# Attention, soft-MoE and FFN on one core: the logits' maximum, two v loads and the first chain change places, and the last first layer goes to fp16 parts

## The chip, the core and the metric

One core of a Trainium2 chip runs the whole program. Its engines are named as the profile names them: PE (TensorE matmul, with PEld for its weight loads), DVE (VectorE), ACT (ScalarE), POOL (GpSimd) and SP (SyncE, which issues nearly all DMAs). The metric is the device time of one execution in microseconds (us).

## The reference

Three layers follow each other on 4608 tokens (8 batches of 576) of 512 features.

```python
# attention: q, k, v of 8 batches x 8 heads x 576 x 64
scores = q @ k.T / sqrt(64);  mask: block of 64 rows sees blocks up to its own
attn = softmax(scores);  x = attn @ v          # 4608 x 512
# soft MoE: phi 512 x 32 slots, 8 experts of 4 slots, w1 512 x 1024, w2 1024 x 512
logits = x @ phi
d = softmax(logits, over the tokens);  slot_input = d.T @ x
slot_out[e] = relu(slot_input[e] @ w1[e]) @ w2[e]
c = softmax(logits, over the slots);   x = c @ slot_out
# FFN: w_in 512 x 2048, w_out 2048 x 512
h = relu(x @ w_in);  out = (h * h) @ w_out
```

The softmax over the tokens runs over all batches, so the kernel keeps a running maximum of the logits for each slot, and rescales what it has summed so far.

## The kernel before

The program goes through five stretches: a start-up (to about 61 us), attention (61 to 425), the experts (to 476), the FFN's first four token tiles (to 545), and the last stage, the other 32 token tiles (to the end).

Attention walks over 32 pairs of heads, four to a batch. In `pair(n)` the scores of pair n, the row maxima of pair n+2 (`maxpass`: PE `ps_max`, DVE `pm` and `ptl`, L498), the products with v of pair n-1 (`pv`: PE `xm` and `tl`), and the scaling and splitting of q and k of pair n+3 (`split`: ACT and DVE write `qa`, `ka`, `qb`, L441 and L447) are interleaved in eight slots. SP then moves `qb` by a transposing DMA (`t<-qb`, L473), `ka` by another, and loads further q, k and v. PE's order in attention is the order in which the code issues its work; that of DVE and ACT comes from a scheduler, within the dependencies. Each engine runs its own queue in order: what waits holds up what is behind it.

The soft-MoE work of batch b-1 is a list of items that the pairs of batch b take one at a time in five of their slots: five `logits` in the second pair of the batch, five more items in the third, and the rest from the fourth on. `logits(u)` ends on POOL (`lg`, `ltl`, L752); `maxes` takes the maximum on DVE (`mxb`, L802 and L803) and copies it (`mx`, L805); `running` transposes it on PE (`ps_mx`, L810) and forms the running maximum and its negative `nm`; `weights` spreads `nm` on PE (`ps_nb`, L821), after which DVE adds it to the logits (`d`, L825 and L826) and ACT takes the exponential (L829, L830); `total` sums `d` on PE (`ps_ds`, L870); `tokens(u)` transposes a tile of attention's output on PE (`ps_x`, L847) and scales it on DVE (`x`, L857). Decoding of FFN weights (`raw`, `dec_sq`, `tin`) runs on DVE and ACT beside it in the batches where it is due.

In the start-up, `prepare` writes constants into `s` on DVE by eleven operations (L294, L300), while the first q and k are squared (ACT `junk`, L382) and summed (PE `ps_ssq`, L389); `chain` turns the sums into scales on DVE (L394 to L411), which ACT's first `ka` needs.

The last stage takes 16 blocks of two token tiles. A block has seven products of 24 fp16 matmuls of 256 columns (L1520) and four groups of `block_first` for the next block: each four fp32 matmuls of 256 columns on the weights `ws` and the inputs `cts` (`ps_hb`, L1484), which ACT (L1375, L1376, L1507) and DVE (L1453, L1497) turn into the fp16 parts of the next block. A string `ORDER` fixes the queues of PE, DVE and ACT from the FFN's fifth part to the end of block 0; behind it PE's order is that of the code.

Of the kernel before, what the change touches and what calls it, by code (L numbers as in the profile page):

```python
# [23 lines left out]
def tile_attn_soft_moe_ffn(  # L24
# [23 lines left out]
    NG = 6  # L48
# [63 lines left out]
    exps = []  # L112

    def after_exp(x):
        if exps:
            tc.add_manual_dep(
                x.ins, exps[-1].ins.name,
                mybir.DependencyInfo(mybir.DependencyClass.NoSync, mybir.DependencyReason.DATA), reason="order",
            )

# [122 lines left out]
    def attention():  # L243
# [132 lines left out]
        def scale(ns, gap=0):  # L376
# [10 lines left out]
            def chain():  # L387
# [334 lines left out]
        def batch(b):  # L722
# [117 lines left out]
            def tokens(u, j0=0, j1=NJ):  # L840
# [9 lines left out]
                if j0 == NJ - 1:  # L850
# [5 lines left out]
                    return  # L856
                nc.vector.tensor_tensor(  # L857
                    out=box[u][0:w].rearrange("p (hp j d) -> p j hp d", hp=2, j=NJ)[:, j0:j1],
# [57 lines left out]
            if b == B - 1:  # L916
# [95 lines left out]
        def pair(n):  # L1012
# [259 lines left out]
    def setup_sel():  # L1272
        sel = c_p.tile([128, 4, 160], F32R, name="sel", bufs=1)
        nc.vector.memset(sel.bitcast(F32), 0.0)
        for i in range(0, 5, 2):
            nc.vector.tensor_copy(sel[:, :, 32 * i:32 * i + 32], ident.rearrange("p (c s) -> p c s", c=4))
        ident_r = c_p.tile([128, 128], F32R, name="ident_r", bufs=1)
        nc.vector.tensor_copy(ident_r, ident)
        cts["sel"], cts["id"] = sel, ident_r
        t = cts["all"] = lo_p.tile([128, 9 * 512], F32R, tag="lo", name="cts")  # L1280
        for g in range(NTILE // NG):
            cts[g] = t[:, NTOK * g:NTOK * g + NTOK]

# [12 lines left out]
    def combine_c(g):  # L1296
        e = lg[:, NG * g:NG * g + NG, :]
        cs = cts["cs_p"].tile([128, NG, 4, NSL], F32R, tag="cs", name="cs", bufs=2)
        for i in range(2):
            nc.vector.tensor_copy(cs[:, :, i, :], e)  # L1300
        for i in range(2, 4):
            nc.vector.tensor_tensor(out=cs[:, :, i, :], in0=e, in1=cs[:, :, 0, :], op=ALU.subtract)
        css[g] = cs

    def combine_b(ps, g):
        pt = ps.bitcast(F32R)
        cs = css.pop(g)
        for i in range(NG):
            nc.tensor.transpose(pt[:, 128 * i:128 * i + 128], cs[:, i].rearrange("p a s -> p (a s)"), cts["id"])
        nc.scalar.copy(cts[g], pt[:, 0:NTOK])  # L1310

    def ffn():
# [65 lines left out]
        def first_hidden(c, step=1024, late=False):  # L1378
# [5 lines left out]
            for a in range(2):  # L1384
# [4 lines left out]
                if step == 512:  # L1389
                    relu_square(ps, g[:, 512 * a:512 * a + 512], 512 * a, 512 * a + 512)  # L1390
                    if a == 0:
                        spread(2, parts[0])
            if late:
                return
            if step == 1024:
                relu_square(ps, g, 0, 1024)
            return g

        def first_square(c, ps):
            g = hid[c] = g_p.tile([128, 1024], F32, tag="g", name="g")  # L1400
            relu_square(ps, g, 0, 1024)

# [22 lines left out]
        def scale_alpha():  # L1425
# [5 lines left out]
                out=se, in0=m2[:, 1:2], scalar=2.0 ** 58, in1=m2[:, 0:1], op0=ALU.mult, op1=ALU.mult  # L1431
            )
            ts(out=se, in0=se, scalar1=2.0 ** -56, scalar2=None, op0=ALU.max)
            ts(out=se.bitcast(U32), in0=se.bitcast(U32), scalar1=MASK, scalar2=None, op0=ALU.bitwise_and)
            ts(out=sg.bitcast(U32), in0=se.bitcast(U32), scalar1=MASK, scalar2=None, op0=ALU.bitwise_xor)
            nc.vector.scalar_tensor_tensor(
                out=sc["alpha"], in0=sg, scalar=2.0 ** 63, in1=h, op0=ALU.mult, op1=ALU.mult
            )
            nc.vector.scalar_tensor_tensor(
                out=sc["inv"], in0=se, scalar=2.0 ** -12, in1=se, op0=ALU.mult, op1=ALU.mult  # L1440
            )

# [35 lines left out]
        def block_first(n, kq):  # L1478
            ps = hbs[n, kq] = bank2("ps_hb")
            c0 = T0 + 256 * n  # L1480
            for j in range(2):
                for a in range(2):
                    f = 2 * kq + j + KH * a
                    nc.tensor.matmul(  # L1484
                        ps[:, 512 * j + 256 * a:512 * j + 256 * a + 256], ws[:, 128 * f:128 * f + 128],
                        ctt[:, c0:c0 + 256], start=True, stop=True,
                    )

        def block_square(n, kq):
            ps = hbs.pop((n, kq))  # L1490
            x = a7[n, kq] = tw["a"].tile([128, 2, 7, 128], F32, tag="a7", name="a7")
            relu_square(ps, x[:, :, 0:4].rearrange("p k a x -> p k (a x)"), 0, 1024, scale=sc["alpha"][:, 0:1])

# [132 lines left out]
        with tc.manual_schedule(engines={E.PE, E.DVE, E.Activation}):  # L1626
# [79 lines left out]
```

## Time and profile before

| | us |
|---|---|
| timed runs, median | 877.38 |
| timed runs, lowest and highest | 873.22, 877.43 |
| profiled execution, its own time | 875.35 |
| profiled execution, span of its instructions | 873.6 |
| PE busy over the span | 818.8 (94%) |
| DVE busy | 668.1 (76%) |
| ACT busy | 625.4 (72%) |
| mean granted clock of TensorE | 0.981 |

An engine's busy time is what its instructions took; its share is taken over the whole span, whose stages have different limits. The rows for the stages and waits stand further below.

### The profile page before, as it was taken

The numbers are of one execution on the slowest core, as the hardware profiler recorded it, in microseconds if no ns is written. First come the engines' busy times: TensorE is split into PE (matmuls) and PEld (weight loads), VectorE is DVE, ScalarE is ACT, GpSimd is POOL, SyncE is SP. The second block draws the span as 40 slices with busy tenths as digits, with TensorE's granted clock in tenths as the row PEclk, the third lists the DMA queues.
The fourth block names the chain that finished last, engine by engine and source line by source line (L and its number), as shares of the span: only waits on it lengthen the run. The fifth ranks groups of instructions, "written<-read, shape, count | busy, mean of one in ns | idle before, by whom it ended". The sixth has DMA issues, their size and how long they took to land.

```text
span 873.6 us, 21610 instructions
## 1 busy us (share of the span) xinstructions
PE 818.8 (94%) x8725; PEld 604.0 (69%) x8725; DVE 668.1 (76%) x1539; ACT 625.4 (72%) x991; POOL 242.9 (28%) x394
## 2 busy tenths in 40 slices
PE   1779999899999999999996999999999999999997
PEld 1446767576666667677432554888898998888887
DVE  5848789989898987764824899788888888888880
ACT  4669787777778777744214889887888888878770
POOL 0236757556475757464000000000000000000000
PEclk9879999999999999999998899999999999999999
DMA  8799898989899987689999300110000000000002
GB/s 150 143 184 181 126 222 153 220 168 212 178 202 190 169 150 160 122 235 310 358 387 387 121 1 0 57 41 26 26 25 26 25 26 25 26 25 26 25 26 49
DMA packets 220356, 113.14 MB, mean 130 GB/s; under 512 B 192096, under 2 KB 194144, under 8 KB 220256
## 3 DMA queue, kind: packets, MB, share of 16 engines
q1 hardware_dynamic: 217600, 111.11, 55.0%
q8 instruction: 68, 1.11, 0.6%
q10 hardware_dynamic: 2656, 0.66, 0.4%
q14 instruction: 32, 0.26, 0.1%
HBM read 78.71 MB, written 9.44 MB: 101 GB/s over the span
## 4 chain that ended last, share of the span: by engine, by line
PE 75%; DMA 8%; POOL 5%; ACT 5%; DVE 3%; issue 2%; SPq 1%; ACTq 0%; POOLq 0%
PE ps_y L1520 14%; PE ps_x L1520 10%; PE ps_z L1520 10%; PE xm L636 7%; PE ps_sc L562 6%; PE po L1542 4%; DMA t<-qb 4%; PE ps_hb L1484 3%; POOL ul L752 2%; PE sm L656 2%; PE ps_max L484 2%; PE ps_u L743 2%; DMA wch<-in_moe_w_dram 2%; POOL ss L605 2%; PE tl L647 2%
## 5 line engine op out<-in xcount | busy, mean ns | idle before, releaser
L1520 PEld LDWEIGHTS <-ah 128*128 128x128 f16 x1792 | 170.4, 98 | 21.5
L600 ACT ACTIVATE p<-ps_sc,es 128x512 f32<-128x512 f32 x192 | 130.1, 686 | 59.8 <-PE ps_sc L562 30.5
L1453 DVE TENSOR_TENSOR al<-a,ah 128x1024 f16<-128x1024 f32 (+1 forms) x128 | 138.6, 1125 | 16.7 <-ACT ah L1507 15.3
L498 DVE TENSOR_REDUCE pm<-ps_max 128x4 f32<-128x512 f32 x160 | 106.5, 684 | 37.0 <-PE ps_max L492 36.8
L605 POOL TENSOR_TENSOR ss<-p 128x384 f32<-128x384 f32 (+1 forms) x128 | 86.0, 690 | 159.6 <-ACT p L600 159.2
L1507 ACT CAST ah<-a 128x1024 f16<-128x1024 f32 (+1 forms) x128 | 114.4, 936 | 14.9 <-DVE a L1453 13.6
L562 PE MATMUL ps_sc<-t,s 128*128 128x512 f16 (+3 forms) x512 | 107.8, 304 | 11.4 <-DMA t<-qb 6.3
L1613 POOL TENSOR_TENSOR ot<-u,p 128x256 f32<-128x256 f32 x16 | 12.5, 783 | 374.6 <-DVE u L1584 358.7
L1520 PE MATMUL ps_y<-bh,ah 128*128 128x256 f16 x384 | 104.8, 273 | 0.0
L1520 PE MATMUL ps_y<-bl,ah 128*128 128x256 f16 x384 | 104.7, 273 | 0.0
L1520 PE MATMUL ps_y<-bh,al 128*128 128x256 f16 x384 | 104.7, 273 | 0.0
L605 POOL TENSOR_TENSOR ss<-ss,p 128x320 f32<-128x320 f32 (+1 forms) x128 | 98.9, 773 | 16.1 <-ACT p L600 8.4
L1375 ACT ACTIVATE r<-ps_hb,alpha 128x1024 f32<-128x1024 f32 x64 | 71.2, 1112 | 33.7 <-PE ps_hb L1484 33.0
L1520 PEld LDWEIGHTS <-al 128*128 128x128 f16 x896 | 87.7, 98 | 10.2
L636 PE MATMUL xm<-p,ar_hi 128*64 128x256 f32 (+3 forms) x512 | 89.0, 447 | 0.0
L1453 DVE TENSOR_TENSOR a<-a 128x256 f32<-128x256 f32 x192 | 76.2, 424 | 3.9
L1520 PE MATMUL ps_x<-bh,ah 128*128 128x256 f16 x256 | 70.1, 274 | 0.0
L1520 PE MATMUL ps_z<-bh,ah 128*128 128x256 f16 x256 | 69.9, 273 | 0.0
L1520 PE MATMUL ps_x<-bl,ah 128*128 128x256 f16 x256 | 69.8, 273 | 0.0
L1520 PE MATMUL ps_x<-bh,al 128*128 128x256 f16 x256 | 69.8, 273 | 0.0
L1520 PE MATMUL ps_z<-bh,al 128*128 128x256 f16 x256 | 69.8, 273 | 0.0
L1520 PE MATMUL ps_z<-bl,ah 128*128 128x256 f16 x256 | 69.8, 273 | 0.0
(257 smaller groups left out, 1788.2 us busy)
## 6 DMA issues: line engine op xcount, KB each, us to landing
wch<-in_moe_w_dram SPq DMA_DIRECT2D x18, 1024.0 KB, 12.8
ar_hi<-in_v_dram SPq DMA_DIRECT2D x64, 128.0 KB, 3.9
raw<-in_moe_w_in_dram SPq DMA_DIRECT2D x16, 512.0 KB, 5.4
out_dram<-ot SPq DMA_DIRECT2D x32, 256.0 KB, 2.2
ar_hi<-in_moe_w_dram SPq DMA_DIRECT2D x6, 1024.0 KB, 8.9
s<-s SPq DMA_DIRECT2D x32, 144.0 KB, 4.0
ar_hi<-in_k_dram SPq DMA_DIRECT2D x16, 256.0 KB, 4.6
ar_hi<-in_q_dram SPq DMA_DIRECT2D x16, 256.0 KB, 4.7
```

The source lines that it names most:

```text
L484: nc.tensor.matmul(ps[:, c0:c0 + 128 * (u + 1)].rearrange("p (s c) -> p s c", c=128), t1[:, 2 * u + hp, :], s1[:, hp:2 * u + 2:2, :], star ...
L498: nc.vector.tensor_reduce(out=o, in_=i, axis=AX.X, op=ALU.max)
L562: nc.tensor.matmul(ps[:, c0:c0 + w].rearrange("p (s c) -> p s c", c=128), kk[:, 2 * t + hp, :], qq[:, 2 * u0 + hp:8:2, :], start=(c0 == 0 ...
L600: exps[:] = [nc.scalar.activation(out=pt, in_=ps, func=AF.Exp, scale=es[:, 0:1])]
L605: add = lambda o, x, y: nc.gpsimd.tensor_tensor(out=o, in0=x, in1=y, op=ALU.add)
L636: nc.tensor.matmul(box["xm"][64 * hp:64 * hp + 64, 128 * t:512], vs[:, t, hp, :], r, start=(t == 0), stop=(t == 3),)
L1375: nc.scalar.activation(out=r[:, c0:c1], in_=ps[:, c0:c1], func=AF.Relu, **kw)
L1453: sub = lambda o, a, b: nc.vector.tensor_tensor(out=o, in0=a, in1=b, op=ALU.subtract)
L1484: nc.tensor.matmul(ps[:, 512 * j + 256 * a:512 * j + 256 * a + 256], ws[:, 128 * f:128 * f + 128], ctt[:, c0:c0 + 256], start=True, stop=True,
L1507: nc.scalar.copy(v(hl[n % 2][0][:, 2 * kq:2 * kq + 2], s), v(a7[n, kq], s))
L1520: nc.tensor.matmul(acc[:, 0:HM], a[:, k], b[:, k], start=bool(first and k + j == 0), stop=(k == KH - 1 and j == 2), skip_group_check=not f ...
L1542: nc.tensor.matmul(pos[t], g[:, 512 * a + 128 * t:512 * a + 128 * t + 128], tt[:, c, a], start=(c == 0 and a == 0), stop=(c == KH - 1 and ...
```

## The change

It has four parts.

1. The constant writes of `prepare` are collected, and the first operation of the first chain (for pair 0) is made to come behind all of them on DVE.
2. The items change places: `tokens(1)` before `maxes`, and then `tokens(2)`, `running`, `tokens(3)`, `weights` in place of `maxes`, `tokens(1)`, `running`, `tokens(2)`, `weights`, `tokens(3)`. So `running` stands one slot later, `weights` one, `tokens(1)` to `tokens(3)` one earlier; `total` keeps its slot. In all batches but the last, `mxb` on DVE comes behind the evacuation of `tokens(1)`'s `x`.
3. In the second pair of a batch no v is loaded; the pair's v is loaded in the third instead, and the third's in the fourth, which loads its own too.
4. The first layer of blocks 2 to 15 takes fp16 inputs and weights: `combine_c` and `combine_b` leave scaled fp16 high and low parts of the inputs, `halves_w` splits the weights, and `spread_w` packs them by 16 fp16 matmuls of 512 columns and two copies of ACT, in the course of block 0. The scale of those blocks' relu changes with it. Blocks 0 and 1 keep fp32.

```diff
@@ ORDER @@
-        "o3 l10 c11 H13 P2 E5 l11 q12 P7 E2 s12 q13 P3 E7 c12 s13 c13 l12 P4 E3 l13 E4"
+        "o3 l10 c11 H13 P2 E5 l11 q12 w P7 E2 s12 q13 W0 P3 E7 c12 s13 W1 c13 l12 P4 E3 l13 E4"
@@ prepare @@
-                    nc.vector.tensor_scalar(out=o, in0=x, scalar1=SHIFT, scalar2=None, op0=ALU.mult)
+                    ready.append(nc.vector.tensor_scalar(out=o, in0=x, scalar1=SHIFT, scalar2=None, op0=ALU.mult))
@@ chain @@
-                nc.vector.tensor_scalar(out=a, in0=a, scalar1=1e-30, scalar2=None, op0=ALU.max)
+                x = nc.vector.tensor_scalar(out=a, in0=a, scalar1=1e-30, scalar2=None, op0=ALU.max)
+                if ns == [0]:
+                    for y in ready:
+                        order(x, y)
@@ batch @@
-                nc.vector.tensor_reduce(out=mxb, in_=lm.rearrange("p u s -> p s u"), axis=AX.X, op=ALU.max)
+                x = nc.vector.tensor_reduce(out=mxb, in_=lm.rearrange("p u s -> p s u"), axis=AX.X, op=ALU.max)
+                if b < B - 1:
+                    order(x, box["x"])
...
-                + [lambda: tokens(0), maxes, lambda: tokens(1), running, lambda: tokens(2), weights, lambda: tokens(3)]
+                + [lambda: tokens(0), lambda: tokens(1), maxes, lambda: tokens(2), running, lambda: tokens(3), weights]
@@ pair @@
-            if n + 2 < N:
-                dq += load_v(n + 2)
+            for m_ in {0: (n + 2,), 1: (), 2: (n + 1,), 3: (n + 1, n + 2)}[jn]:
+                if m_ < N:
+                    dq += load_v(m_)
@@ combine_c @@
-        cs = cts["cs_p"].tile([128, NG, 4, NSL], F32R, tag="cs", name="cs", bufs=2)
+        cs = cts["cs_p"].tile([128, NG, 4, NSL], F16, tag="cs", name="cs", bufs=2)
@@ ffn @@
+        wfs = cts["w"][:, p]
         nc.scalar.copy(wfs, psw[:, p])
+        nc.scalar.copy(cts["w"][:, parts[0]], psw[:, parts[0]])
...
+        def halves_w():
...
+            wh = cts["wh"].rearrange("p (i f) -> p i f", i=2)
+            nc.scalar.activation(out=wh[:, 0], in_=cts["w"], func=AF.Copy, scale=sw)
+            nc.vector.scalar_tensor_tensor(
+                out=wh[:, 1], in0=cts["w"], scalar=sw, in1=wh[:, 0], op0=ALU.mult, op1=ALU.subtract
+            )
+
+        def spread_w(k):
+            ps = bank2("ps_wh")
+            for c in range(2):
+                for i in range(4):
+                    nc.tensor.matmul(
+                        ps[32 * i:32 * i + 32, 512 * c:512 * c + 512], cts["id_h"][:, 64 * c + 32 * k:64 * c + 32 * k + 32],
+                        cts["wh"][:, 512 * (i % 2):512 * (i % 2) + 512], start=True, stop=True, tile_position=(0, 32 * i),
+                    )
+            nc.scalar.copy(
+                cts["ws"].rearrange("p (c k f) -> p c k f", c=2, k=2)[:, :, k], ps.rearrange("p (c f) -> p c f", c=2)
+            )
...
+            w, c = (ws, ctt[:, c0:c0 + 256]) if n < 2 else (cts["ws"], cts["half"][:, c0 - CT0:c0 - CT0 + 256])
             for j in range(2):
                 for a in range(2):
                     f = 2 * kq + j + KH * a
                     nc.tensor.matmul(
-                        ps[:, 512 * j + 256 * a:512 * j + 256 * a + 256], ws[:, 128 * f:128 * f + 128],
-                        ctt[:, c0:c0 + 256], start=True, stop=True,
+                        ps[:, 512 * j + 256 * a:512 * j + 256 * a + 256], w[:, 128 * f:128 * f + 128], c,
+                        start=True, stop=True,
                     )
```

What this does to the queues is seen at three places. Line numbers are those of the kernel that the rows are from; from the chain on, those of the changed kernel are 7 to 12 higher. The first place is DVE's queue in the start-up, where `cst` and `s` are the constants and `ps_ssq` the sums of the first chain; before:

```order
L293 TENSOR_TENSOR cst<-ident 64x1
L394 TENSOR_SCALAR ps_ssq<-ps_ssq 128x2
L294 SCALAR_TENSOR_TENSOR cst<-ident,cst 64x6
L300 TENSOR_SCALAR s_0_144<-cst 64x8x64
...
L300 TENSOR_SCALAR s_1_145<-cst 64x4x64
L395 TENSOR_SCALAR ps_ssq<-ps_ssq 128x2
```

And of the change:

```order
L300 TENSOR_TENSOR cst<-ident 64x1
L301 SCALAR_TENSOR_TENSOR cst<-ident,cst 64x6
L307 TENSOR_SCALAR s_0_144<-cst 64x8x64
...
L307 TENSOR_SCALAR s_1_145<-cst 64x4x64
L401 TENSOR_SCALAR ps_ssq<-ps_ssq 128x2
L405 TENSOR_SCALAR ps_ssq<-ps_ssq 128x2
```

The chain's first operation has moved behind all eleven constant writes, and its second follows it directly.

The second place is DVE's queue in the third pair of batch 2, where the work of batch 1 is taken up; before:

```order
L802 TENSOR_REDUCE mxb<-lg 128x32
L447 SCALAR_TENSOR_TENSOR qb_142<-ar_hi,sig,qa 128x9x64
L803 TENSOR_TENSOR mxb<-mxb,ltl 64x32
L805 COPY mx_2754<-mxb 128x128
L498 TENSOR_REDUCE pm_146<-ps_max 128x4
L498 TENSOR_REDUCE ptl<-ps_max 128x4
...
L857 TENSOR_TENSOR x<-ps_x,rc 128x4x2x64
L189 SCALAR_TENSOR_TENSOR tin<-dec_sq,raw 128x512
L498 TENSOR_REDUCE pm_146<-ps_max 128x4
L195 TENSOR_SCALAR dec_sq<-tin 128x512
```

And of the change:

```order
L457 SCALAR_TENSOR_TENSOR qb_142<-ar_hi,sig,qa 128x9x64
L508 TENSOR_REDUCE pm_146<-ps_max 128x4
L508 TENSOR_REDUCE ptl<-ps_max 128x4
...
L869 TENSOR_TENSOR x<-ps_x,rc 128x4x2x64
L508 TENSOR_REDUCE pm_146<-ps_max 128x4
L196 SCALAR_TENSOR_TENSOR tin<-dec_sq,raw 128x512
L812 TENSOR_REDUCE mxb<-lg 128x32
L508 TENSOR_REDUCE pm_146<-ps_max 128x4
L815 TENSOR_TENSOR mxb<-mxb,ltl 64x32
L202 TENSOR_SCALAR dec_sq<-tin 128x512
L817 COPY mx_2773<-mxb 128x128
```

`mxb` and `mx` have moved from ahead of eleven operations to behind them. On PE, `ps_mx` has changed places with the group of `ps_x` that followed it directly.

The third place is ACT's queue in the fourth pair of that batch, with the exponentials of `d`; before:

```order
L600 ACTIVATE p<-ps_sc,es 128x512
L382 ACTIVATE junk,ssq<-ar_hi 128x576
L829 ACTIVATE d<-d 64x32
L830 ACTIVATE d<-d 128x128
L600 ACTIVATE p<-ps_sc,es 128x512
L382 ACTIVATE junk,ssq<-ar_hi 128x576
L600 ACTIVATE p<-ps_sc,es 128x512 x2
```

And of the change:

```order
L610 ACTIVATE p<-ps_sc,es 128x512
L389 ACTIVATE junk,ssq<-ar_hi 128x576
L610 ACTIVATE p<-ps_sc,es 128x512
L389 ACTIVATE junk,ssq<-ar_hi 128x576
L841 ACTIVATE d<-d 64x32
L610 ACTIVATE p<-ps_sc,es 128x512
L842 ACTIVATE d<-d 128x128
L193 ACTIVATE dec_sq<-raw 128x512
```

Another `p` and `junk` stand ahead of the first `d`, and a `p` between the two. On PE, `ps_nb`, which `d` waits for, has changed places with the last full group of `ps_x`, and `ps_ds`, which waits for `d`, stands where it stood.

## Rows read from the trace of the kernel before

**Rows 1.** Windows by stage: length, busy of PE, PEld, DVE, ACT, POOL, PEclk, DMA.

```profile
61.00:425.00 364.00, 351.59 (x4881) 243.82 (x4877) 292.55 (x788) 266.30 (x542) 215.76 (x353) 1.00 0.95 193
545.00:873.00 328.00, 324.12 (x2932) 290.71 (x2930) 251.57 (x426) 249.61 (x292) 12.53 (x16) 1.00 0.09 30
```

**Rows 2.** Waits of PE, 60 to 430 us: total us, times, longest.

```profile
PE ps_sc L562 <- DVE pm L498: 4.7, 4, 1.7
PE ps_sc L562 <- DMA t<-qb: 3.6, 5, 1.6
PE ps_ssq L389 <- ACT p L600: 1.1, 5, 0.2
```

**Rows 3.** Timeline of DVE at the start: start, us, instruction, idle before it.

```profile
11.68 0.17 DVE L394 TENSOR_SCALAR ps_ssq<-ps_ssq 128x2 f32<-128x2 f32 x1 [6.32 <-PE ps_ssq L389]
...
11.83 2.00 DVE L300 TENSOR_SCALAR s<-cst 64x512 f16<-64x512 f32 x10
```

**Rows 4.** Timeline of PE, 46 to 52 us.

```profile
50.97 0.38 PE L389 MATMUL ps_ssq<-ssq,ones 128*128 128x2 f32 x2 [3.15 <-ACT junk L382]
```

**Rows 5.** Timeline of DVE, 150 to 170 us.

```profile
152.49 0.37 DVE L802 TENSOR_REDUCE mxb<-lg 128x32 f32<-128x128 f32 x1
...
154.34 0.23 DVE L805 COPY mx<-mxb 128x128 f32<-128x128 f32 x1
154.49 0.68 DVE L498 TENSOR_REDUCE pm<-ps_max 128x4 f32<-128x512 f32 x1
...
160.41 0.16 DVE L533 TENSOR_REDUCE ps_max<-pm 128x4 f32<-128x16 f32 x1
```

**Rows 6.** Timeline of PE, 155 to 175 us.

```profile
155.22 0.59 PE L562 MATMUL ps_sc<-t,s 128*128 128x512 f16 x2 [0.62 <-DVE pm L498]
...
158.05 0.28 PE L810 MATMUL ps_mx<-ident,mx 128*128 128x128 f32 x1
...
165.22 0.40 PE L821 MATMUL ps_nb<-ident,nm 32*128 32x32 f32 x2
...
167.01 0.66 PE L847 MATMUL ps_x<-ident,xt 128*128 128x128 f32 x4
...
168.28 0.39 PE L870 MATMUL ps_ds<-ones,d 128*32 128x1 f32 x10
...
173.58 0.38 PE L562 MATMUL ps_sc<-t,s 128*128 128x512 f16 x1 [1.62 <-DMA t<-qb]
```

**Rows 7.** Timeline of ACT, 164 to 171 us.

```profile
166.86 0.68 ACT L382 ACTIVATE junk<-ar_lo 128x576 fp8e4<-128x576 f32 x1
...
167.65 0.30 ACT L830 ACTIVATE d<-d 128x128 f32<-128x128 f32 x1
167.84 0.67 ACT L600 ACTIVATE p<-ps_sc,es 128x512 f32<-128x512 f32 x1
```

**Rows 8.** Timeline of SP's DMA issues, 149 to 176 us.

```profile
164.46 1.50 SPq L312 DMA_DIRECT2D ar_hi<-in_v_dram  x1
...
167.70 1.56 SPq L473 DMA_TRANSPOSE t<-qb  x1
```

**Rows 9.** Timeline of PE in a block of the last stage, 599 us on.

```profile
599.75 0.27 PE L1520 MATMUL ps_y<-bl,ah 128*128 128x256 f16 x1
```

**Rows 10.** Timeline of all engines around a first-layer group, 606.8 to 608.2 us.

```profile
607.07 0.27 PE L1520 MATMUL ps_y<-bh,al 128*128 128x256 f16 x1
...
607.10 0.71 PE L1484 MATMUL ps_hb<-cts,ws 128*128 128x256 f32 x4
...
607.77 0.27 PE L1520 MATMUL ps_x<-bl,ah 128*128 128x256 f16 x1
```

**Rows 11.** Timeline of PE in the expert stage, 471 to 475 us.

```profile
472.45 1.92 PE L1183 MATMUL psw<-tin,so 128*32 128x512 f32 x16 [0.28 <-DVE so L1176]
```

**Rows 12.** Timeline of ACT at the start of the FFN.

```profile
474.44 0.27 ACT L1349 CAST wf<-psw 128x128 fp32r<-128x128 f32 x1 [2.59 <-PE psw L1183]
```

**Rows 13.** Windows in the start-up, same columns as in rows 1.

```profile
56.00:61.00 5.00, 5.00 (x34) 2.41 (x36) 2.96 (x17) 4.03 (x8) 2.05 (x3) 0.50 1.29 217
```

More of the change, by code (lines that the diff above doesn't have):

```diff
@@ L64, in tile_attn_soft_moe_ffn @@
     NTOK = 128 * NG
+    CT0 = 128 * N0 + 512
+    CSC = 2.0 ** 15
     KF = FF // 128
@@ L112, in tile_attn_soft_moe_ffn, with order @@
     exps = []
+    def order(x, y):
+        tc.add_manual_dep(
+            x.ins, y.ins.name,
+            mybir.DependencyInfo(mybir.DependencyClass.NoSync, mybir.DependencyReason.DATA), reason="order",
+        )
+    ready = []
     def after_exp(x):
         if exps:
[L116 to L119, printed above, removed]
+            order(x, exps[-1])
     def qk_tile(b):
@@ L856, in tokens @@
                     return
-                nc.vector.tensor_tensor(
+                box["x"] = nc.vector.tensor_tensor(
                     out=box[u][0:w].rearrange("p (hp j d) -> p j hp d", hp=2, j=NJ)[:, j0:j1],
@@ L1276, in setup_sel @@
             nc.vector.tensor_copy(sel[:, :, 32 * i:32 * i + 32], ident.rearrange("p (c s) -> p c s", c=4))
[L1277 to L1282, printed above, removed]
+        cts["sel"] = sel
+        cts["all"] = c_p.tile([128, CT0], F32R, name="cts", bufs=1)
+        t = lo_p.tile([128, 9 * 512], F32, tag="lo", name="cts_h")
+        n_h = NT - CT0
+        cts["half"] = t[:, 0:n_h // 2].bitcast(F16)
+        t = t[:, n_h // 2:]
+        cts["ws"], cts["wh"] = t[:, 0:FF // 2].bitcast(F16), t[:, FF // 2:FF // 2 + 512].bitcast(F16)
+        cts["id_h"] = t[:, FF // 2 + 512:FF // 2 + 576].bitcast(F16)
+        nc.vector.tensor_copy(cts["id_h"], ident)
+        c0 = FF // 2 + 1088
+        cts["w"] = t[:, c0 - 512:c0]
+        cts["tiny"] = [t[:, c0 + i:c0 + i + 1] for i in range(4)]
     def combine_a(g):
@@ L1297, in combine_c @@
         e = lg[:, NG * g:NG * g + NG, :]
-        cs = cts["cs_p"].tile([128, NG, 4, NSL], F32R, tag="cs", name="cs", bufs=2)
+        cs = cts["cs_p"].tile([128, NG, 4, NSL], F16, tag="cs", name="cs", bufs=2)
         for i in range(2):
-            nc.vector.tensor_copy(cs[:, :, i, :], e)
+            nc.vector.tensor_scalar(out=cs[:, :, i, :], in0=e, scalar1=CSC, scalar2=None, op0=ALU.mult)
         for i in range(2, 4):
-            nc.vector.tensor_tensor(out=cs[:, :, i, :], in0=e, in1=cs[:, :, 0, :], op=ALU.subtract)
+            nc.vector.scalar_tensor_tensor(
+                out=cs[:, :, i, :], in0=e, scalar=CSC, in1=cs[:, :, 0, :], op0=ALU.mult, op1=ALU.subtract
+            )
         css[g] = cs
     def combine_b(ps, g):
-        pt = ps.bitcast(F32R)
+        pt = ps.bitcast(F16)
         cs = css.pop(g)
         for i in range(NG):
-            nc.tensor.transpose(pt[:, 128 * i:128 * i + 128], cs[:, i].rearrange("p a s -> p (a s)"), cts["id"])
-        nc.scalar.copy(cts[g], pt[:, 0:NTOK])
+            nc.tensor.transpose(pt[:, 128 * i:128 * i + 128], cs[:, i].rearrange("p a s -> p (a s)"), cts["id_h"])
+        c0 = NTOK * g
+        n = max(0, min(NTOK, CT0 - c0))
+        if n:
+            nc.scalar.copy(cts["all"][:, c0:c0 + n], pt[:, 0:n])
+        if n < NTOK:
+            nc.scalar.copy(cts["half"][:, c0 + n - CT0:c0 + NTOK - CT0], pt[:, n:NTOK])
     def ffn():
@@ L1332, in ffn @@
         sc = {nm: ws_p.tile([128, 1], F32, name=nm) for nm in ("beta", "alpha", "inv", "sg", "se")}
+        sc.update(zip(("top", "sw"), cts["tiny"][2:]))
+        al = [sc["alpha"]] + cts["tiny"][:2]
         wf = [d_p.tile([128, 512], F32R, name=f"wf{i}", bufs=1) for i in range(2)]
-        wfs = d_p.tile([128, 384], F32, name="wfs", bufs=1)
         tt = t_p.tile([128, KH, 2, DM], F32, name="t")
@@ L1389, in first_hidden @@
                 if step == 512:
-                    relu_square(ps, g[:, 512 * a:512 * a + 512], 512 * a, 512 * a + 512)
+                    relu_square(ps, g[:, 512 * a:512 * a + 512], 512 * a, 512 * a + 512, scale=1.0 / CSC)
                     if a == 0:
@@ L1395, in first_hidden @@
             if step == 1024:
-                relu_square(ps, g, 0, 1024)
+                relu_square(ps, g, 0, 1024, scale=1.0 / CSC)
             return g
@@ L1400, in first_square @@
             g = hid[c] = g_p.tile([128, 1024], F32, tag="g", name="g")
-            relu_square(ps, g, 0, 1024)
+            relu_square(ps, g, 0, 1024, scale=1.0 / CSC)
         tw = {}
@@ L1432, in scale_alpha @@
             )
+            ts(out=sc["top"], in0=m2[:, 0:1], scalar1=2.0 ** -100, scalar2=None, op0=ALU.max)
             ts(out=se, in0=se, scalar1=2.0 ** -56, scalar2=None, op0=ALU.max)
@@ L1438, in scale_alpha @@
             )
+            ts(out=al[1], in0=al[0], scalar1=1.0 / CSC, scalar2=None, op0=ALU.mult)
             nc.vector.scalar_tensor_tensor(
                 out=sc["inv"], in0=se, scalar=2.0 ** -12, in1=se, op0=ALU.mult, op1=ALU.mult
+            )
+        def halves_w():
+            top, sw = sc["top"], sc["sw"]
+            ts(out=top.bitcast(U32), in0=top.bitcast(U32), scalar1=MASK, scalar2=None, op0=ALU.bitwise_and)
+            ts(out=sw.bitcast(U32), in0=top.bitcast(U32), scalar1=MASK, scalar2=None, op0=ALU.bitwise_xor)
+            ts(out=sw, in0=sw, scalar1=2.0 ** 13, scalar2=None, op0=ALU.mult)
+            nc.vector.scalar_tensor_tensor(
+                out=al[2], in0=top, scalar=2.0 ** -14 / CSC, in1=al[0], op0=ALU.mult, op1=ALU.mult
+            )
+            wh = cts["wh"].rearrange("p (i f) -> p i f", i=2)
+            nc.scalar.activation(out=wh[:, 0], in_=cts["w"], func=AF.Copy, scale=sw)
+            nc.vector.scalar_tensor_tensor(
+                out=wh[:, 1], in0=cts["w"], scalar=sw, in1=wh[:, 0], op0=ALU.mult, op1=ALU.subtract
+            )
+        def spread_w(k):
[5 more added lines that the diff above has]
+                        cts["wh"][:, 512 * (i % 2):512 * (i % 2) + 512], start=True, stop=True, tile_position=(0, 32 * i),
+                    )
+            nc.scalar.copy(
+                cts["ws"].rearrange("p (c k f) -> p c k f", c=2, k=2)[:, :, k], ps.rearrange("p (c f) -> p c f", c=2)
             )
@@ L1491, in block_square @@
             x = a7[n, kq] = tw["a"].tile([128, 2, 7, 128], F32, tag="a7", name="a7")
-            relu_square(ps, x[:, :, 0:4].rearrange("p k a x -> p k (a x)"), 0, 1024, scale=sc["alpha"][:, 0:1])
+            relu_square(ps, x[:, :, 0:4].rearrange("p k a x -> p k (a x)"), 0, 1024, scale=al[2 if n > 1 else 1][:, 0:1])
         def block_sums(n, kq):
@@ L1648, in ffn @@
                 "X": block_open,
+                "w": halves_w,
+                "W": spread_w,
             }
```

## Prediction

> **What bounds the kernel now.** I read the table of stretches first [rows 1]. The reader is to see two stages that matter here. In attention (61 to 425 us) PE, the TensorE matmul queue, is busy 351.6 of 364 us; DVE, the VectorE, 292.6, ACT, the ScalarE, 266.3, and the DMA share is 0.95. So only some 12 us of PE's time there are idle, and that is all that a better order can win. In the last stage (545 to 873) PE is busy 324.1 of 328 us, ACT 249.6 and DVE 251.6: PE's own instructions are the time, and whatever ACT and DVE get on top has room. Next come PE's waits in attention [rows 2]: 4.7 us in four waits for a `pm` reduction of DVE (L498), 3.6 us in five for the transposed load `t<-qb`, 1.1 us in five for `p` at the sums of squares. Then I read the timelines of DVE, ACT, SP and PE where the change moves something.
>
> The sum is made against the profiled execution, 875.35 us (span 873.6, the rest lies outside it). The median of the timed runs is 877.38, and the profiled one lies between their lowest and highest, 873.22 and 877.43. A difference under 0.5% (4.4 us) can hardly be told from none.
>
> **First chain behind the set-up.** DVE has nothing to do for 6.32 us until the first `ps_ssq` arrives at 11.68, runs the first operation of the chain (L394), and then ten constant writes of 2.00 us before the second [rows 3]. Written first, they fall into the 6.32 us that it waits. What is won is their 2.00 us less some 0.1 of overlap at the ends: **-1.9 us**. Behind it ACT's `ka` and the first transposes start earlier, and the chain of the start-up runs on PE's waits up to 50.97 (PE waited 3.15 us there [rows 4]); if the loads of the start bind and not this chain, the gain is 0. I take 1.9.
>
> **The maximum of the logits later.** Each pair of heads has five slots for the work of the batch before; `running` (PE's transpose `ps_mx`, L810) moves one slot later, `weights` (PE `ps_nb`, L821) one too, the `x` transposes of tiles 1 to 3 one earlier, and `total` (PE `ps_ds`, L870) stays. Removed: in one batch DVE reduces `mxb` at 152.49 and then has to wait for GpSimd's last sum before it copies `mx` at 154.34; `pm` follows at 154.49 [rows 5], and PE, which needs that `pm`, stood 0.62 us until 155.22 [rows 6]. Without the wait in DVE that stand goes, 4.7 us in all. But two new waits stand in the order, and both are PE's, behind which everything on PE queues.
>
> *`ps_mx` behind `mx`.* Before, `mx` was ready 3.7 us ahead of its use (154.34 and 158.05 [rows 5, 6]). Now `mx` stands behind eleven operations of DVE that stood behind it. Those ran back to back from 154.49 to 160.41, 5.92 us [rows 5]. They can begin when `qb` is done, 0.7 us after 152.49, at about 153.2; with the reduction, the small maximum and the copy between them (0.3, 0.1 and 0.15) `mx` is done at 159.7, and up to 160.1 where DVE waits for PE's `ps_max` and `ps_x`. PE, 0.62 us ahead of before and with one group of four transposes (0.6) moved ahead of `ps_mx`, is there at 158.0. It stands 1.7 to 2.1 us. Against before, when PE had both groups done 0.9 us after 158.05 and then lost 0.2 to `t<-qb`, this is a loss of 0.8 to 1.2. Where the old wait was 1.7 us [rows 2] it comes out at about nothing. In the first and the last such batch no decoding stands between, but the evacuation of `x` does; by the same count 0.5 to 1.4 each. Six batches: two at 1.0, two at 0, two at 1.0: +4, bounds +1.5 and +5.
>
> *`ps_ds` behind `d`.* Before, PE issued `ps_nb` at 165.22 and `ps_ds` at 168.28, 3.06 us later, and ACT had written the larger `d` by 167.95 (167.65 and 0.30) [rows 6, 7]. Now `ps_nb` stands where the last transposes stood (167.01 [rows 6]), 1.3 us ahead of `ps_ds`. ACT's order is `junk`, `p`, `junk`, `d`, `p`, `d`: behind the second `junk`, which ends at 167.5, stand a `p` (0.6 with the overlap of its end), a `junk` (0.7), the small `d` (some 0.1), a `p` (0.6) and the larger `d` (0.3) [rows 7]: 169.8, and PE is at `ps_ds` at 168.3 [rows 6]. That is 1.5 us in each of six batches, or 1.0 if ACT, with nothing to wait for, runs half a microsecond ahead. Part is no loss, since PE was to wait soon after: 1.1 us for `p` and, by their places, 3.1 of the 3.6 us for `t<-qb` [rows 2] (1.62 at 173.58 alone [rows 6]). So 9.0 or 6.0 less 4.2: +4.8 or +1.8.
>
> Together +3.3 to +9.8 for the attention stage; if neither wait appeared, all that is left is the old waits removed, 4.7 + 3.6 = -8.3. Rows and order speak for the waits; DVE and ACT have more idle time once PE stands, so I take a value in the lower half, **+6.0**.
>
> **Loads of v.** In the second pair of a batch two issues of SP, the queue of the loads, fall away, and in the third pair two of four; the last pair has six for two. One took 1.50 us at 164.46, and the transposed load `t<-qb` that PE waited for at 173.58 was issued at 167.70 behind it [rows 6, 8]; with two such issues fewer ahead it can go up to 3 us earlier, and I take 1.5 for the pair. Its profit is the 3.6 us of waiting, which the `ps_ds` wait covers anyway, so I count nothing more; v itself is used a pair later, so it still comes in time. If those issues weren't hidden in the last pair, at most four times 1.50 us a batch would stand ahead of the next `t<-qb`; since PE will stand at `ps_ds` and `ps_mx` anyway, I count none of it, and a full +6 in one batch is no likelier than the -3.6. The Trainium skill (DMA: Bandwidth & Descriptors, section Issuing engines are not separate DMA queues) says that the time to initiate a DMA is usually small relative to the DMA itself: by it their order would hardly matter, and the term would be nothing at all. Here an issue took 1.50 us, so the trace doesn't quite agree; by the row the term would be up to -3.6 with no other wait in PE's way. The sum is the same by both.
>
> **Last stage from fp16 parts.** A matmul of a product starts every 0.1093 us (599.75 to 607.07 in 67 steps [rows 9, 10]). Around the four fp32 matmuls of a first-layer group, from the last product before (607.07) to the second behind (607.77), 0.70 us pass [rows 10]; six steps of 0.1093 would be 0.656. So a group gains 0.044 us, if fp16 runs at the products' pace; four groups in each of 14 blocks: **-2.5 us**. Bounds: 0, if the pace doesn't change, and -5.0, twice it, if the fp32 weight loads delay more than these two steps show. The Trainium skill (TensorE: Matmul & The Clock Gate, section Weight-path perf modes) has the fast weight load on for 128 weights that are not FP32; the rows agree in sign, fp32 loads being slower, and hidden but for the 0.044.
>
> Added on PE are 16 fp16 matmuls of 512 columns that pack the weights. The trace has 16 fp32 ones in 32-column groups in 1.92 us [rows 11]; at half that, which the lighter type suggests, 1.0 us, and up to 3.4 if they run one after another at twice the 256-column pace above (16 times 0.2186). I take **+1.0**. The scales and halves on DVE and the copies of ACT lie beside PE, in the 76 us or more that each has free [rows 1]; without that cover one copy would cost some 1 us, once. One more copy of a 128x128 corner stands on ACT's path at the start of the FFN; the like took 0.27 [rows 12]: **+0.25**. The fp16 split of the first layer's inputs lies under the loads of the expert stage.
>
> **Sum.** -1.9 + 6.0 + 0 - 2.5 + 1.0 + 0.25 = +2.85: 878.2 us.
>
> **Rivals.** *The new waits don't appear* (faster). ACT and DVE had idle time just ahead of both places, and if they come 1.5 us earlier, the old waits go and nothing follows: 875.35 - 1.9 - 8.3 - 1.25 = 863.9; at half of the low reading's way from -8.3 to +3.3 it is 869.7. For it: PE waited 4.7 us for DVE exactly because of `mxb`. Against: DVE ran back to back from 154.49 to 160.41 [rows 5], so a copy put behind that is late. *The waits lower PE's clock* (slower). After PE's 3.15 us without work ahead of 50.97 the granted clock was 0.50, the lower of the two levels, over 56 to 61 us, while it stayed at 1.00 over all of attention with its waits up to 1.7 us [rows 1, 2, 4, 13]. A new wait over 2.1 us, between the two, could do it; each time costs at least half of 5 us, 2.5. In two batches that is +5 on the sum: 883. Against: PE works right before and behind. *The fp16 part does nothing* and the packing costs 3.4: +3.65 in place of -1.25, 883 too. For it: the weight loads are beside the matmuls already; against: the 0.70 us. *Nothing of the start-up counts*: 880.
>
> **Chances.** The forecast as summed, 875 to 882: 0.6. The new waits absent or small: 0.24. Clock or fp16 part, beyond 882: 0.16. Of the first, a fifth lies above 879.7 (slower). So faster by over 0.5% 0.24, within it 0.48, slower 0.28. The range that holds 8 in 10 is 867 to 884; for the forecast alone 875 to 882.
>
> **What would show it.** The chain: DVE's constant writes ahead of its first `ps_ssq`, and ACT's first `ka` some 1.9 us earlier. The order: new lines of PE's waits, `ps_mx` for `mx` and `ps_ds` for `d`, of 1 to 2 us in six batches each, and the line for `pm` gone. The loads: `t<-qb` earlier behind the second pair. The last stage: blocks from the third on 0.18 us shorter. The prediction is wrong if PE's idle time in attention falls under 12 us, if the clock drops there, or if a group of the first layer still takes 0.70.

## The result, and the profile after

The changed kernel took 886.74 us (median; 882.43 to 889.63), the kernel before 875.3 beside it: a ratio of 1.0138 (95% interval 1.0107 to 1.0168), slower by some 12 us. The prediction, 878.2 and at most 884, was too low; the largest share of its chance, 0.48, lay within 0.5% of no difference, and 0.28 on slower.

Where the time went is read first from the stretches, as in [rows 1]. Windows of the changed kernel's profiled execution (span 886.1 us), with the same columns:

```profile
61.00:425.00 364.00, 341.79 (x4710) 235.29 (x4711) 284.04 (x750) 258.20 (x520) 219.99 (x350) 0.98 0.91 181
545.00:873.00 328.00, 327.56 (x2902) 285.71 (x2903) 264.50 (x443) 264.80 (x306) 11.80 (x15) 1.00 0.08 29
```

In attention PE was busy 9.8 us less in the same 364 us, and the granted clock, 1.00 before, is 0.98. To compare like with like, the stretch from PE's first logits (`ps_u`) to its last serves better, since its work is the same. The kernel before:

```profile
94.00:385.70 291.70, 281.76 (x3915) 195.71 (x3912) 247.50 (x645) 221.19 (x443) 181.47 (x300) 1.00 0.95 178
```

And the changed kernel:

```profile
91.40:395.70 304.30, 284.42 (x3914) 196.06 (x3913) 246.83 (x645) 219.84 (x443) 187.18 (x300) 0.98 0.90 170
```

The stretch begins 2.6 us earlier and lasts 12.6 us longer. PE's idle time grew from 9.9 (291.70 less 281.76) to 19.9, and the same matmuls kept it busy for 2.7 us more. Outside it the spans differ by little: 2.1 us more from the last logits to the start of `psw` in the expert stage, 1.3 more from there to the first `ps_hb`, 0.8 less through the last stage.

The answer to [rows 2] is the table of PE's waits, 60 to 440 us, of the changed kernel:

```profile
PE ps_ds L882 <- ACT d L842: 9.5, 7, 1.5
PE ps_mx L822 <- DVE mx L817: 6.7, 5, 1.7
PE ps_mx L822 <- DVE ps_max L543: 4.9, 2, 2.6
PE ps_max L494 <- DMA s<-ka: 2.3, 1, 2.3
```

The waits for `pm`, `t<-qb` and `p` are gone, and the two that the prediction found in the order stand in their place. The releaser `ps_max` in the third line is the operation right behind the copy `mx` on DVE. In six batches the new waits are 8.3 us at `ps_ds` (1.5 in each of five, 0.7 in the sixth) and 11.2 at `ps_mx` (1.3 to 2.6 each). The seventh wait at `ps_ds`, 1.2 us, lies behind the last logits and is part of the 2.1 us above. One batch shows both. PE's timeline, where [rows 6] had neither:

```profile
162.22 0.30 PE L822 MATMUL ps_mx<-ident,mx 128*128 128x128 f32 x1 [2.56 <-DVE ps_max L543]
...
170.27 0.40 PE L833 MATMUL ps_nb<-ident,nm 32*128 32x32 f32 x2
...
172.99 0.20 PE L882 MATMUL ps_ds<-ones,d 128*32 128x1 f32 x2 [1.53 <-ACT d L842]
```

ACT's timeline, in answer to [rows 7], shows what `ps_ds` waited for: `p`, `junk`, the small `d`, another `p`, and only then the larger `d`.

```profile
170.71 0.68 ACT L610 ACTIVATE p<-ps_sc,es 128x512 f32<-128x512 f32 x1
171.28 0.68 ACT L389 ACTIVATE junk<-ar_lo 128x576 fp8e4<-128x576 f32 x1
...
171.95 0.22 ACT L841 ACTIVATE d<-d 64x32 f32<-64x32 f32 x1
172.07 0.68 ACT L610 ACTIVATE p<-ps_sc,es 128x512 f32<-128x512 f32 x1
172.64 0.30 ACT L842 ACTIVATE d<-d 128x128 f32<-128x128 f32 x1
```

The clock is seen in windows of four microseconds, behind the `ps_ds` waits of three of the batches:

```profile
124.00:128.00 4.00, 4.00 (x24) 1.44 (x18) 2.92 (x14) 1.12 (x2) 1.07 (x2) 0.67 0.53 146
...
176.00:180.00 4.00, 4.00 (x28) 1.84 (x26) 2.88 (x14) 1.88 (x3) 0.40 (x1) 0.77 1.01 269
...
226.00:230.00 4.00, 4.00 (x24) 1.35 (x17) 3.07 (x15) 0.98 (x2) 1.32 (x2) 0.62 0.82 227
```

PE is busy all the time in these windows, at a mean between the two levels, 1.2 and 2.4 GHz.

At the start the constants are written where they were meant to go. DVE's timeline, in answer to [rows 3]:

```profile
5.48 2.00 DVE L307 TENSOR_SCALAR s<-cst 64x512 f16<-64x512 f32 x10
11.11 0.17 DVE L401 TENSOR_SCALAR ps_ssq<-ps_ssq 128x2 f32<-128x2 f32 x1 [3.63 <-PE ps_ssq L396]
```

In the last stage a first-layer group now runs at the products' pace. PE's timeline, in answer to [rows 10]:

```profile
624.55 0.27 PE L1578 MATMUL ps_x<-bh,al 128*128 128x256 f16 x1
624.66 0.60 PE L1542 MATMUL ps_hb<-cts_h 128*128 128x256 f16 x4
625.10 0.27 PE L1578 MATMUL ps_y<-bh,ah 128*128 128x256 f16 x1
```

From the last product before the group to the first behind it 0.55 us pass, five steps of 0.11.

### The profile page after: what moved, and what is told of

The parts are those of the page before. It is cut to its first block, busy times and chain, and to the rows that moved or that the text cites. A ratio compares the mean times of both kernels' runs of the same rounds, so it can differ in the third digit from the quotient of the medians.

```text
span 886.1 us, 21643 instructions
## 1 busy us (share of the span) xinstructions
PE 819.0 (92%) x8741; PEld 598.3 (68%) x8741; DVE 669.1 (76%) x1546; ACT 626.1 (71%) x996; POOL 248.7 (28%) x394
## 4 chain that ended last, share of the span: by engine, by line
PE 68%; DMA 10%; DVE 9%; ACT 7%; issue 3%; SPq 2%; ACTq 0%; POOL 0%
PE ps_y L1578 14%; PE ps_z L1578 9%; PE ps_x L1578 9%; PE xm L646 6%; PE ps_sc L572 5%; PE ps_hb L1542 3%; DMA raw<-in_moe_w_in_dram 2%; PE ps_u L753 2%; PE po L1600 2%; PE ps_max L494 2%; PE sm L666 2%; DMA wch<-in_moe_w_dram 2%; ACT p L610 2%; DVE pm L508 2%; PE ps_h L1224 2%
## 5 line engine op out<-in xcount | busy, mean ns | idle before, releaser
L1578 PEld LDWEIGHTS <-ah 128*128 128x128 f16 x1792 | 174.8, 98 | 21.9 <-issue 0.8
L615 POOL TENSOR_TENSOR ss<-p 128x384 f32<-128x384 f32 (+1 forms) x128 | 89.8, 720 | 157.7 <-ACT p L610 157.5
L1565 ACT CAST ah<-a 128x1024 f16<-128x1024 f32 (+1 forms) x128 | 114.4, 936 | 15.0 <-DVE a L1510 13.4
L1404 ACT ACTIVATE r<-ps_hb,cts_h 128x1024 f32<-128x1024 f32 x64 | 71.2, 1112 | 30.0 <-PE ps_hb L1542 29.4
L646 PE MATMUL xm<-p,ar_hi 128*64 128x256 f32 (+3 forms) x512 | 87.2, 440 | 0.0
```

What stands on the lines that cost most here:

```text
L615: add = lambda o, x, y: nc.gpsimd.tensor_tensor(out=o, in0=x, in1=y, op=ALU.add)
L646: nc.tensor.matmul(box["xm"][64 * hp:64 * hp + 64, 128 * t:512], vs[:, t, hp, :], r, start=(t == 0), stop=(t == 3),)
L1404: nc.scalar.activation(out=r[:, c0:c1], in_=ps[:, c0:c1], func=AF.Relu, **kw)
L1565: nc.scalar.copy(v(hl[n % 2][0][:, 2 * kq:2 * kq + 2], s), v(a7[n, kq], s))
L1578: nc.tensor.matmul(acc[:, 0:HM], a[:, k], b[:, k], start=bool(first and k + j == 0), stop=(k == KH - 1 and j == 2), skip_group_check=not f ...
```

## The experiments

There were two theories and a third that may come with the first. O: the new order of the soft-MoE items costs two waits of PE. V: the later loads of v disturb the transfers. K: the waits also lower PE's clock. All ratios are to the kernel before on the same chip, with 95% intervals.

**The order alone, and everything but the order.** The first takes the new line of items and the dependency of `mxb` into the kernel before; the second puts the old ones back into the changed kernel.

```diff
-                + [lambda: tokens(0), maxes, lambda: tokens(1), running, lambda: tokens(2), weights, lambda: tokens(3)]
+                + [lambda: tokens(0), lambda: tokens(1), maxes, lambda: tokens(2), running, lambda: tokens(3), weights]
```

> Before with only the new order of the soft-MoE items (running, weights one slot later, mxb behind x of tile 1). Theory O (two new waits of PE, ps_mx for mx and ps_ds for d, some 20 us in all, against some 9 us of old waits that they cover): +9 to +14 us, with about 9 us of waits at ps_ds and 11 at ps_mx as after the change. Rival V (the later loads of v slow the transfers): -2 to +3 us. Rival K (the clock falls after the new waits): as O, and the granted clock under 0.9 in several stretches of attention; the waits alone would explain less than the loss.

> The changed kernel with the old order of the items, so first chain, v loads and fp16 parts alone. Theory O: -2 to -6 us against before, with the waits for pm back (4.7 us) and no line for ps_mx or ps_ds. Rival V: +6 to +12 us, as after the change.

Measured: the order alone 1.0276 (1.0246 to 1.0306), 24 us slower, twice the whole change; all but the order 0.9917 (0.9885 to 0.9949), some 7 us faster than before, the fastest of all and a little beyond the range expected. V falls: the other parts help. O holds in sign and place, but the loss is above its range. The order alone, waits of PE from 61 to 410 us:

```profile
PE ps_mx L817 <- DVE mx L812: 16.3, 6, 3.3
PE ps_ds L877 <- ACT d L837: 8.3, 6, 1.5
```

The `ps_mx` waits are 5 us longer than in the changed kernel, and between its first and last logits (93.4 to 406.9) PE was idle 24.6 us and busy 288.9, 7.2 more than before, with the granted clock at 0.97. So K is at work too. The window:

```profile
93.40:406.90 313.50, 288.92 (x3916) 198.22 (x3913) 250.37 (x645) 220.57 (x443) 183.47 (x300) 0.97 0.89 165
```

**The two halves of the order.** One kernel moves only `weights` behind `tokens(3)`, the other only `maxes` and `running`.

```diff
-                + [lambda: tokens(0), maxes, lambda: tokens(1), running, lambda: tokens(2), weights, lambda: tokens(3)]
+                + [lambda: tokens(0), maxes, lambda: tokens(1), running, lambda: tokens(2), lambda: tokens(3), weights]
```

```diff
-                + [lambda: tokens(0), maxes, lambda: tokens(1), running, lambda: tokens(2), weights, lambda: tokens(3)]
+                + [lambda: tokens(0), lambda: tokens(1), maxes, lambda: tokens(2), running, weights, lambda: tokens(3)]
```

> Before with only weights one item later (behind tokens 3), maxes and running where they were. Theory O: six waits of 1.5 us at ps_ds, 9 us, less 1.1 for the sums of squares and up to 3.1 for t<-qb that they cover: +5 to +8 us; no wait at ps_mx. Rival K: the clock stays at 1.00, since 1.5 us is under the 1.7 that left it so before. If a wait of 1.5 us is made good elsewhere: 0 to +2.

> Before with only maxes and running one item later (and mxb behind x of tile 1), weights where it was. Theory O: waits at ps_mx of 1.3 to 2.6 us in six batches, 11 us, less 4.7 for pm and 0.5 for t<-qb: +4 to +7 us; no wait at ps_ds, unless nm comes too late for ps_nb. Rival K: granted clock under 0.9 behind the longest of these waits (2.3 and 2.6 us), worth up to 3 us more.

Measured: 1.0098 (1.0065 to 1.0131) and 1.0149 (1.0115 to 1.0182); the two add up to 1.0247, near the 1.0276 of both. Each has only its own wait (8.3 us at `ps_ds`, 16.7 at `ps_mx`, where 11 was expected, up to 3.4). Both lost more than the waits explain. With `weights` later, PE's idle time grew by 3.8 us and its busy time by 3.9, from the first to the last logits:

```profile
93.40:392.80 299.40, 285.67 (x3916) 196.69 (x3913) 247.70 (x645) 221.51 (x443) 181.30 (x300) 0.98 0.91 173
```

That kernel refutes what the expectation said of the clock, that a wait of 1.5 us would leave it alone. PE's timeline and the windows around it:

```profile
170.38 0.39 PE L870 MATMUL ps_ds<-ones,d 128*32 128x1 f32 x10 [1.52 <-ACT d L830]
```

```profile
168.00:172.00 4.00, 2.48 (x37) 1.79 (x40) 2.18 (x7) 2.96 (x10) 2.39 (x4) 1.00 1.19 242
172.00:176.00 4.00, 4.00 (x18) 1.28 (x12) 3.88 (x19) 2.48 (x6) 1.79 (x2) 0.57 1.09 217
```

The clock fell in the same way behind the waits that ended at 269.87 and 320.61, and not behind equal ones at 122.18 and 221.11. So it isn't one length of wait that decides. In the window with the wait PE was busy for 2.48 of 4 us.

**The waits filled.** In the changed kernel, 12 idle matmuls stand ahead of `ps_mx` and of `ps_ds`.

```diff
+                if b < B - 1:
+                    spin(ps[:, 256:512], 12)
...
+                if b < B - 1:
+                    spin(ds[:, 256:512], 12)
```

> The changed kernel, with 12 idle matmuls of 256 columns (some 1.3 us, into unused columns of the same tiles, no work left out) ahead of ps_mx and of ps_ds in all batches but the last, so that PE is busy through most of the two new waits and nothing else moves. Theory K (the waits also let PE's granted clock fall, and that is part of the loss): no stretch of attention under 1.00, and 3 to 6 us less than the changed kernel, so +6 to +9 against before. If the waits alone are the loss: the same as the changed kernel or, where the matmuls are longer than the wait, up to 2 us more: +11 to +14.

Measured: 1.0109 (1.0079 to 1.0139) where the changed kernel had 1.0138 (1.0107 to 1.0168); these overlap, so the profile has to tell. Its window from the first to the last logits:

```profile
92.30:392.00 299.70, 295.37 (x4058) 208.54 (x4057) 246.30 (x645) 220.14 (x443) 187.27 (x300) 1.00 0.93 173
```

144 matmuls of 0.109 us are 15.7 us of this busy time. Without them PE is busy some 279.7 and waiting or filling some 20.0, as long as the changed kernel's 19.9 idle; but the clock is at 1.00 and the stretch is 4.6 us shorter. So by this pair of profiled executions the clock is 4.6 of the 12.6 us, and the waits the rest. PE's busy time gives less, 2.7 us more in the changed kernel than before; we take the clock's part to lie between the two. The timed ratios, 0.3% apart, agree but don't prove it alone. The granted clock of the timed runs, a mean over the whole program, bears it out: 0.976 to 0.982 in the four of the changed kernel, 0.984 to 0.986 in the six with the waits filled.

**The sum of d one slot later.** In the changed kernel `total` moves behind `tokens(4)`.

```diff
-                + [total, lambda: [gather(u) for u in range(4)], lambda: tokens(4), lambda: gather(4)]
+                + [lambda: tokens(4), total, lambda: [gather(u) for u in range(4)], lambda: gather(4)]
```

> The changed kernel with the sum of d (ps_ds) behind the transposes of tile 4, one slot further from ps_nb. Theory O (the distance from ps_nb to ps_ds is what was taken away): the waits at ps_ds, 8.3 us in six batches, fall under 2, and with them some of the clock's loss: 6 to 11 us less than the changed kernel, so +1 to +6 against before. Rival: the wait moves to the products with d behind it (ps_dx) or to the next pair, and less than 3 us are won.

Measured: 1.0049 (1.0027 to 1.0072), some 8 us less than the changed kernel. The distance was the cause of this wait. Waits of PE from 90 to 400 us:

```profile
PE ps_mx L822 <- DVE mx L817: 6.6, 4, 1.8
PE ps_mx L822 <- DVE ps_max L543: 6.0, 2, 3.2
PE ps_dx L908 <- ACT p L610: 2.5, 4, 0.6
PE ps_ds L882 <- ACT d L842: 0.3, 1, 0.3
```

What is left at `ps_ds` is 0.3 us; the clock falls in one batch in place of three.

**A wide order.** The maximum stays late, and all that follows it is moved along: `tokens(3)` and then `running`, `tokens(4)`, `weights`, two empty places, `total`.

```diff
-                + [lambda: tokens(0), lambda: tokens(1), maxes, lambda: tokens(2), running, lambda: tokens(3), weights]
-                + [total, lambda: [gather(u) for u in range(4)], lambda: tokens(4), lambda: gather(4)]
+                + [lambda: tokens(0), lambda: tokens(1), maxes, lambda: tokens(2), lambda: tokens(3), running]
+                + [lambda: tokens(4), weights, lambda: None, lambda: None]
+                + [total, lambda: [gather(u) for u in range(4)], lambda: gather(4)]
```

> The changed kernel with the maximum still late, but what follows it moved along: running two places later than before the change, weights three, total five (behind the transposes of tile 4, in the pair after). Theory O: mx, nm and d are all ready when PE comes to them, so neither the old waits for pm (4.7 us) nor the new ones at ps_mx (11.2) and ps_ds (8.3) stand: -1.2 to -1.8% against before, some 4 us less than all but the order (0.9917); granted clock at 1.00 through attention. Rival: what DVE no longer does early is late somewhere else (d at ps_ds, x at ps_dx, the next batch's logits), and it is no better than all but the order.

Measured: 0.9932 (0.9908 to 0.9955). The old waits and the new ones are gone and the clock stays up, but it is no better than all but the order. So the rival was right in what it said of the time, though not of the place: at `ps_ds` and `ps_dx`, which it named, 0.2 us each are left. Waits of PE from 90 to 400 us:

```profile
PE sm L666 <- POOL ss L615: 4.5, 4, 1.2
PE ps_nb L833 <- DVE nm L827: 2.8, 6, 0.5
```

PE now waits for GpSimd's sums of `p`, and for `nm` a little in each of six batches.

**The other parts one by one.** Each goes alone into the kernel before: the loads of v (the lines of the diff in `pair`), first chain and fp16 parts together, the chain, the fp16 parts.

> Before with only the loads of v later. If the waits for t<-qb (3.6 us) go, as the issue of v stood in their way: -2 to -4 us. If the transfers share the DMA engines all the same: 0, or +1 where six issues in the last pair push the next transposed load back.

> Before with only the first chain behind the set-up and the fp16 parts. By the prediction's terms -1.9 and -1.25: -3 us, with blocks 3 to 15 each 0.18 us shorter. If the fp16 parts do nothing: 0 to +1. What is missing to the -6.6 of all but the order is then the v loads'.

> Before with only the first chain behind the set-up. By the prediction -1.9 us; the first logits on PE, at 93.4 to 94.6 us in the kernels without it and at 90.2 to 92.3 in those with it, say -2.5. If the loads of the start bind: 0.

> Before with only the fp16 parts. By the prediction -2.5 for the groups, +1.0 for the packing, +0.25 for the copy: -1.25 us. By the profiles so far the groups of blocks 2 to 15 gain 2.3 and block 0 with the packing is 1.5 longer: -0.8, with the stage's other parts as before. If all of chain and fp16 together (0.9971) is the fp16 parts': -2.5.

Measured: v 0.9971 (0.9949 to 0.9992), its waits for `t<-qb` from 90 to 400 us down from 3.6 to 0.4 us; chain and fp16 together 0.9971 (0.9947 to 0.9995); the chain alone 0.9996 (0.9971 to 1.0020); the fp16 parts alone 0.9997 (0.9972 to 1.0023). The last two apart give less than together; the intervals leave room for both, and no more can be said of so small a gain than that it is between nothing and 0.5%. The loads of v and this pair add up to 0.6%, where all but the order has 0.8%; the intervals leave room for that too. The line left at `t<-qb` with the loads of v alone:

```profile
PE ps_sc L562 <- DMA t<-qb: 0.4, 1, 0.4
```

**The order with the loads of v.** Both go into the kernel before.

> Before with the new order of the items and the later loads of v. If the later loads take from the new order's loss (order alone 1.0276, whole change 1.0138): 1.015 to 1.02, with the waits at ps_mx at 11 to 13 us in place of 16.3. If chain and fp16 make up the difference: 1.023 to 1.028, with the waits at ps_mx still at 16.

Measured: 1.0174 (1.0142 to 1.0207), with 11.1 us at `ps_mx`, as the first of the two expectations had it. So the later loads take 1.0% from the order's loss, three times what they are worth alone. What differs is on DVE, in the third pair of batch 3. With the order alone:

```profile
211.72 1.19 DVE L194 SCALAR_TENSOR_TENSOR tin<-dec_sq,raw 128x512 f32<-128x512 f32 x1 [0.40 <-ACT dec_sq L191]
...
213.72 0.35 DVE L810 TENSOR_TENSOR mxb<-mxb,ltl 64x32 f32<-64x32 f32 x1
...
214.34 0.63 DVE L812 COPY mx<-mxb 128x128 f32<-128x128 f32 x1
```

And with the loads of v too:

```profile
212.23 0.69 DVE L194 SCALAR_TENSOR_TENSOR tin<-dec_sq,raw 128x512 f32<-128x512 f32 x1
...
213.72 0.17 DVE L810 TENSOR_TENSOR mxb<-mxb,ltl 64x32 f32<-64x32 f32 x1
...
214.16 0.21 DVE L812 COPY mx<-mxb 128x128 f32<-128x128 f32 x1
```

The three operations take 1.1 us less, all of it ahead of `ps_mx`. The three together are shorter in four of the six batches, by 3.5 us in all, while the waits at `ps_mx` are 5.2 us shorter in all six. PE's busy time from the first to the last logits is 3.4 us less too, with four falls of the clock in place of six. In the first kernel GpSimd's sums of `p` ran back to back beside the three, and the small `mxb` and `mx` ended within 0.1 us of the end of such a sum. The Trainium skill (SBUF — State Buffer, section Who interferes with whom) says that a DVE instruction with two SBUF inputs contends with a GpSimd instruction that reads SBUF, because the second input comes through a read interface that both share. `tin` and `mxb` have two such inputs, and the rows of the first kernel agree with it; `mx`, a copy, has one. In the second kernel `tin` lay almost wholly in a gap of 0.62 us between sums, but sums ran beside `mxb` and `mx` there too, and why they didn't hold them up wasn't tried. How the loads of v bring this about stays open.

## Why the prediction was wrong

**The waits were right, the sum of them was not.** The prediction worked out 1.7 to 2.1 us at `ps_mx` and 1.5 at `ps_ds`; the trace has 1.3 to 2.6 and 1.5. It netted these against the old waits at +3.3 to +9.8, with +8.8 by its own two terms, and then took +6.0, "a value in the lower half", because DVE and ACT would have idle time once PE stands. That step failed. PE's idle time grew by 9.9 us, just above the top of the range: nothing was given back. The `d` of each batch hangs on `ps_nb` and so moves with PE. The runs show it: the wait at `ps_ds` was 1.5 us in five batches and 0.7 in the sixth both with `weights` alone later, where PE never waited at `ps_mx`, and with the order alone, where it waited there for up to 3.3 us first.

**The clock was taken for a rival when it came with the forecast.** It was given a wait of over 2.1 us as its condition, two batches, and no place in the sum: this is the second step that failed. The granted clock fell in three batches of the changed kernel, behind waits of 1.5 us at `ps_ds`, while waits of 2.3 and 2.6 us at `ps_mx` left it at 1.00. The three falls cost 2.7 us by PE's busy time and 4.6 by the filled waits, so 0.9 to 1.5 each, where 2.5 was said. That the rival's +5 comes near is luck, since too few falls met too high a price. As a term of the sum, 8.8 for the waits and 2.7 to 4.6 for the clock are 11.5 to 13.4, where the stretch grew by 12.6. The clock's drop in attention is one of the signs of being wrong that the prediction gave.

**The loads of v were counted at nothing.** Alone they are worth 0.3%, with `t<-qb` no longer waited for as forecast; with the order they are worth 1.0%, in part by DVE's shorter operations, which the prediction didn't see. So they took from the loss and did not cause it.

**The first chain.** ACT's first `ka` came 2.4 us earlier (0.6 of it because the first sums were earlier too), and the stretch of logits began 2.6 us earlier in the changed kernel. Over the kernels here the first logits came at 90.2 to 93.0 us with the new chain and at 92.6 to 94.7 without it, in the mean 1.9 us apart. But alone the chain gained nothing that shows, 0.9996 (0.9971 to 1.0020), an interval that holds both the 1.9 taken and the bound of 0. With the chain alone PE waits 2.4 us for the transposed `s<-ka` near 60 us, where the kernel before doesn't, which fits the loads as the limit; but with the loads of v alone, and with the fp16 parts alone, it waits 1.8 there too, so what the chain is worth isn't settled.

**The last stage.** Blocks from the third on: from the first group of block 2 to the last matmul of block 15's groups 271.2 us pass in place of 273.5, a gain of 2.3 (2.5 forecast). The packing made the stretch ahead of it, block 0's first group to block 2's, 52.9 in place of 51.6 us, +1.4 (1.0 forecast, inside its bounds). The copy at the start of the FFN took 0.27 us, as forecast. Together these are -0.6, and the fp16 parts alone measure as no difference. The 1.3 us more between `psw` and the last stage don't belong to the change alone: the same span was 43.8 to 46.9 us over the kernels here.

## What to carry to other kernels

When work on a queue is moved one place, list for each consumer how many microseconds lie between it and its producer before and after, on every engine in between: where a moved producer keeps its old consumer, the distance that was cover becomes a wait. Count such waits in full unless a row shows what gives the time back. And count with them what an idle TensorE costs afterwards: in this case the clock took some 3 to 5 of the 12.6 us and the waiting the rest, and moving one consumer along by one slot gave 8 us back.

## What was not expected of the hardware

The granted clock fell behind 12 of the 20 waits of 1.5 us at `ps_ds` (changed kernel, order alone, `weights` alone, order with the loads of v). At `ps_mx` it fell behind all nine waits of 2.9 to 3.4 us (order alone, maximum alone, sum of d later) and behind none of the 21 waits of 1.3 to 2.8 us there (the same three, the changed kernel, and order with the loads of v). In the kernel before it stayed at 1.00 behind waits of 1.7 us [rows 2]. So the length of the wait alone doesn't decide, and what else does wasn't tried.

A copy of 128x128 on DVE took 0.21 us in one kernel and 0.63 in another, a `tin` of 128x512 0.69 and 1.19, with the same DVE instructions from `tin` to the copy.
